# Opening of a fused attention and two-layer kernel: softmax sums of two units in column tiles spread by transfers, score banks paired, squares folded on GpSimd

## The chip, the core and the metric

The kernel runs on one core of a Trainium2 chip. Its engines work in parallel, each through its own instructions in order: TensorE (PE: matmuls; PEld: its weight loads), VectorE (DVE), ScalarE (ACT), GpSimd (POOL) and SyncE (SP, which here only starts transfers). Sixteen DMA engines move data; those transfers that SP starts stand in the profile as queue q1, those that GpSimd starts as q0. The metric is device time in microseconds (us); less is better.

## The reference

Attention over 8 batches and 12 heads, 448 rows of 64 each, with q and k normalized first; then a layer pair with a leaky rectifier between.

```python
q_n, k_n = rmsnorm(q, g_q), rmsnorm(k, g_k)        # x / sqrt(mean(x*x) + 1e-6) * g
scores = scale * np.matmul(q_n, k_n.transpose(0, 1, 3, 2))
scores = scores - np.max(scores, axis=-1, keepdims=True)
attn = np.exp(scores)
attn = attn / (np.sum(attn, axis=-1, keepdims=True) + 1e-09)
x = np.matmul(attn, v)          # then laid out as 3584 x 768
h = x @ w_in                    # 768 x 2048
out = np.maximum(0.01 * h, h) @ w_out   # 2048 x 768
```

## The kernel before

**Units.** The work is cut into 24 units of four heads, three units to a batch. A unit u goes through these steps, each a small function:

- `load(u)` (L146): q and k, 448 KB each, started by SP into `raw` tiles (three buffers); `load_v` (L149) v, `load_w_in` (L125) and `load_w_out` (L128) the weights, started by GpSimd, which also converts them to 16 bits.
- `prep_sqp` (L173) squares q and k on GpSimd (`prep_sq`, L169, on ScalarE), `prep_ssq` (L180) sums the squares of each row on VectorE, `prep_rinv` (L185, L186) makes 1/rms with Ln and Exp on ScalarE, `prep_norm` (L192) multiplies on VectorE.
- `tr` or `trn` (L861, L204) transposes on TensorE, with copies back by VectorE (L809, L811).
- `qk(u, steps)` (L222): seven score steps of four 64x64 matmuls, each into a pair of PSUM banks; `ex(u)` (L242) is the exponential of a step, from PSUM into the tile `et`, on ScalarE. It takes a shift, `eb`, so that nothing overflows: `shift_max` takes the maximum of step 0 on VectorE, `shift_mm` spreads it over the partitions with a matmul.
- `zsum`/`zsum_slot` (L300, L311) sum the exponentials with matmuls by ones, `zinv` turns the sums into reciprocals in the tile `rz` with Ln and Exp (L385, L387); `pv` (L401) multiplies the exponentials by v; `xmul` (L410) multiplies that by `rz` on VectorE and frees the banks of `pv`.
- For units 3 to 22 the sums are made in another form: `zcol` (L338) leaves them in four column tiles of 32 partitions, `zcol_ln` and `zcol_inv` (L359, L364) work on 224 columns into the tile `zs`, and four transfers of SP (L369) spread `zs` over the partitions of `rz`.

`zs` and `rz` come from `zpool`, which has one buffer of each; `zcol_ln` of the next unit writes the `zs` that the transfers before it read, and the next `rz` is the one that `xmul` before it reads.

**The order.** The schedule is manual: each engine gets its instructions in the order of the program. Units 0 to 2 are written out by hand (L828 to L1029), and this is the opening. From unit 3 on a loop interleaves the scores of a unit with matmuls of the two layers, from a plan. The eight PSUM banks are kept in a list: `slot` gives a pair of the banks 4 to 7 to a score step, `aux` a single one of the banks 0 to 3 (in the opening); `drop` gives them back. `warm(n, bank)` (L825) issues n matmuls of ones whose result nothing reads.

In the opening, between the score steps of unit 1 stand the sums and values of unit 0 (`zsum_slot(0)`, `pv(0)`, `zinv(0)`, `xmul(0)`) and the normalizing of unit 2; between those of unit 2 the same of unit 1 and unit 3. `pv(2)` takes the two banks that `pv(1)` had. `gate(u)` (L288) is a tiny copy on GpSimd that waits for the normalized k of unit u, so that what follows on GpSimd doesn't run ahead.

Of the kernel before, what the change touches and what calls it, by code (L numbers as in the profile page):

```python
# [8 lines left out]
FP32 = mybir.dt.float32  # L9
FP16 = mybir.dt.float16  # L10
AF = mybir.ActivationFunctionType
ALU = mybir.AluOpType
# [6 lines left out]
def kernel(  # L19
# [41 lines left out]
    def mine(i):  # L61
        return shared or i < 4

    def aux():
        can = [i for i in free if mine(i)]
        if shared:
            can = [i for i in can[:-1] if i ^ 1 not in free] or can
        free.remove(can[0])
        return single[can[0]]
# [12 lines left out]
    def drop(tile_):  # L82
        for i in range(8):
            if tile_ is single[i]:
                assert i not in free
                free.append(i)
                return
        x = [i for i in range(4) if tile_ is double[i]][0]
        assert 2 * x not in free and 2 * x + 1 not in free
        free.extend((2 * x, 2 * x + 1))  # L90
# [31 lines left out]
    def load_w_in(n0, n):  # L122
        for a in range(2):
            for r in range(2):
                nc.gpsimd.dma_start(win16[64 * a:64 * a + 64, :, r, n0:n0 + n], win_v[a, :, :, r, n0:n0 + n])  # L125
# [22 lines left out]
    def load_v(u):  # L148
        nc.gpsimd.dma_start(vts[u % NV].rearrange("p a t d -> p a (t d)"), rows(v, u))  # L149
# [9 lines left out]
    def buf(u, name):  # L159
        if name not in st[u]:  # L160
            shape, dtype, bufs = SHAPES[name]
            st[u][name] = prep_p.tile(shape, dtype, tag=name[:2] if bufs == 3 and name != "qkT" else name, bufs=bufs, name=name)
        return st[u][name]
# [7 lines left out]
    def prep_sqp(u, tis=BOTH):  # L171
        for ti in tis:
            nc.gpsimd.tensor_tensor(buf(u, f"sq{ti}"), raw[u][ti], raw[u][ti], op=ALU.mult)  # L173

    def prep_g(u):
        nc.vector.tensor_scalar(buf(u, "qkT")[:, 0], buf(u, "qkT")[:, 0], gcol, None, op0=ALU.mult)

    def prep_ssq(u, c=ALL, tis=BOTH):
        for ti in tis:
            nc.vector.tensor_reduce(buf(u, "ssq")[:, ti, :, c[0]:c[1]], buf(u, f"sq{ti}")[:, :, c[0]:c[1]],  # L180
                                    axis=AXL.X, op=ALU.add)

    def prep_rinv(u, tis=BOTH):
# [35 lines left out]
    def score(u, t, banks):  # L219
        for r in range(2):  # L220
            for a in range(2):
                nc.tensor.matmul(banks[a][64 * r:64 * r + 64, 0:S].rearrange("p (t x) -> p t x", t=NS),  # L222
                                 kT(u, r, a, t), qT(u, r, a), start=True, stop=True)

    def qk(u, steps):
        st[u]["sT"] = []
        for t in steps:
            sT = slot()
            score(u, t, (sT[:, 0], sT[:, 1]))
            st[u]["sT"].append((t, sT))  # L230

    def ex(u, most=NS):
        s = st[u]
        if "et" not in s:
            s["et"] = epool.tile([P, NS, 2, S], FP16, tag="et", name="et")
        for t, sT in s["sT"][:most]:
            if isinstance(sT, list):
                for a in range(2):
                    nc.scalar.activation(s["et"][:, t, a], sT[a][:, 0:S], AF.Exp, bias=s["eb"], scale=1.0)
                    drop(sT[a])  # L240
            else:
                nc.scalar.activation(s["et"][:, t], sT[:, :, 0:S], AF.Exp, bias=s["eb"], scale=1.0)  # L242
                drop(sT)
        s["sT"] = s["sT"][most:]

    def score0(u):
        banks = [aux() for a in range(2)]
        score(u, 0, banks)
        st[u]["sT"] = [(0, banks)]

    def shift_max(u):
        s = st[u]
        sT = s["sT"][0][1]
        if isinstance(sT, list):
            pm2 = small.tile([P, 2], FP32, tag="pm2", name="pm2")
            for a in range(2):
                nc.vector.tensor_reduce(pm2[:, a:a + 1], sT[a][:, 0:S], axis=AXL.X, op=ALU.max)
            s["spare"] = sT[0]
            nc.vector.tensor_reduce(s["spare"][:, 511:512], pm2, axis=AXL.X, op=ALU.max)
        else:  # L260
            s["spare"] = sT[:, 0]
            nc.vector.tensor_reduce(s["spare"][:, 511:512], sT[:, :, 0:S], axis=AXL.XY, op=ALU.max)  # L262
        s["dg"] = small.tile([P, P], FP16, tag="dg", name="dg")
        nc.vector.tensor_tensor(s["dg"], ident16, s["spare"][:, 511:512].broadcast_to([P, P]), op=ALU.mult)

    def shift_bank(u):
        st[u]["pb"] = aux()

    def shift_mm(u):
        s = st[u]  # L270
        if u > 0 and "pslot" in st[u - 1]:
            pb = st[u - 1]["pslot"][:, :, S:S + 64]
            for x in range(2):
                nc.tensor.matmul(pb[:, x], onesp, s["dg"][:, 64 * x:64 * x + 64], start=True, stop=True)  # L274
            nc.vector.tensor_reduce(s["spare"][:, 510:511], pb, axis=AXL.XY, op=ALU.max)  # L275
        else:
            if "pb" not in s:
                shift_bank(u)
            pb = s["pb"]
            nc.tensor.matmul(pb[:, 0:P], onesp, s["dg"], start=True, stop=True)  # L280
            nc.vector.tensor_reduce(s["spare"][:, 510:511], pb[:, 0:P], axis=AXL.X, op=ALU.max)
            if u >= 3:
                drop(pb)
        s["eb"] = small.tile([P, 1], FP32, tag="eb", name="eb")
        nc.vector.tensor_scalar(s["eb"], s["spare"][:, 510:511], -1.0, DELTA, op0=ALU.mult, op1=ALU.add)

    def gate(u):
        nc.gpsimd.tensor_copy(gate_t, buf(u, "n16")[:, 1, NS - 1, 1, D - 1:D])  # L288
# [534 lines left out]
    def warm(n, bank):  # L823
        for x in range(n):
            nc.tensor.matmul(bank[:, P:2 * P], onesp, onesp, start=True, stop=True)  # L825

    with tc.manual_schedule():
# [25 lines left out]
        prep_norm(0, K0, (1,))  # L853
        prep_norm(0, K1, (1,))

        def tr(u, ti, chunks, tp=None):
            if tp is None:
                tp = aux()
            for c, copy in chunks:
                for x in range(*c):  # L860
                    nc.tensor.transpose(as_tp(tp)[:, x, :], buf(u, "n16")[:, ti, x].rearrange("p a d -> p (a d)"), ident16)  # L861
                copy(buf(u, "qkT")[:, ti, c[0]:c[1]], as_tp(tp)[:, c[0]:c[1]], ti == 0)
            return tp
# [12 lines left out]
        gate(0)  # L876
        load_v(0)
        prep_sqp(2, (0,))
        load_v(1)
        load_v(2)  # L880
        load_w_in(0, 1024)
        shift_bank(0)
        warm(10, st[0]["pb"])
# [4 lines left out]
        def trn(u, ti, copy):  # L888
            prep_tr(u, ti, ((ALL, copy),))
# [14 lines left out]
        gate(1)  # L904
        prep_sqp(2, (1,))
        prep_sqp(3, (0,))
        load_w_in(1024, 1024)
        wb = aux()
        warm(12, wb)
# [3 lines left out]
        drop(wb)  # L913
        qk(0, (3,))
        ex(0)
        drop(tr(1, 0, ((ALL, vcopy),)))
        tpk = tr(1, 1, ((K0, vcopy),))
        qk(0, (4,))
        ex(0)
        k1 = []  # L920
# [3 lines left out]
        shift_max(1)  # L924
        vcopy(*k1[0])
        drop(tpk)
        shift_bank(1)
        qk(0, (5,))
        ex(0)
        warm(8, st[1]["pb"])  # L930
        qk(0, (6,))
        ex(0)
        warm(4, st[1]["pb"])
        shift_mm(1)
        prep_ssq(2, ALL, (1,))
        prep_ssq(3, ALL, (0,))
        ex(1)
        prep_rinv(2)
        qk(1, (1,))
        ex(1)  # L940
        zsum_slot(0)
        pv(0)
        zinv(0)
        prep_norm(2)
        gate(2)
        prep_sqp(3, (1,))
        load_v(3)
        load(5)
        prep_sqp(4, (0,))
        load_v(4)  # L950
        for f in range(2):
            load_w_out(8 * f, 8)
        qk(1, (2,))
        warm(6, st[1]["pb"])
        drop(st[1]["pb"])
        ex(1)
        trn(2, 0, vcopy)
        qk(1, (3,))
        ex(1)
        trn(2, 1, vcopy)  # L960
        xmul(0)
        qk(1, (4,))
        ex(1)
        qk(1, (5,))
        ex(1)
        score0(2)
        shift_max(2)
        qk(1, (6,))
        ex(1)
        shift_bank(2)  # L970
        warm(12, st[2]["pb"])
        shift_mm(2)
        prep_ssq(3, ALL, (1,))
        prep_ssq(4, ALL, (0,))
        ex(2)
        prep_rinv(3)
        qk(2, (1,))
        ex(2)
        zsum_slot(1)
        pv(1)  # L980
        zinv(1)

        prep_norm(3)
        load(6)
        gate(3)
        prep_sqp(4, (1,))
        prep_sqp(5)
        load_v(5)
        qk(2, (2,))
        ex(2)  # L990
        warm(12, st[2]["pb"])
        qk(2, (3,))
        ex(2)
        drop(st[2]["pb"])
        trn(3, 0, vcopy)
        warm(8, st[2]["pb"])
        trn(3, 1, vcopy)
        xmul(1)
        prep_ssq(4, ALL, (1,))
        qk(2, (4,))  # L1000
        ex(2)
        st[2]["zt"] = [aux() for r in range(2)]
# [14 lines left out]
        moe1_part(0, first, 0, 2)  # L1017
        shift_mm(3)
        xmul(2, (1,))
        push(0)  # L1020
        moe1_part(0, first, 2, KT - 2)
        ex(3)
# [147 lines left out]
```

## Time and profile before

| what | value |
|---|---|
| median of 3 runs | 409.96 us (408.93 to 411.95) |
| the profiled execution | 410.29 us, of it a span of 408.3 us from first to last instruction |
| PE, DVE, ACT, POOL busy | 395.0, 307.4, 301.4, 74.0 us |
| exponential of a score step (L242, 128x896) | 1.015 us, 166 times |
| Ln and Exp of the sums, wide (L385, L387) | 0.91 and 0.95 us, 3 times each |
| Ln and Exp of the sums, column tiles (L359, L364) | 0.36 and 0.40 us, 20 times each |
| sum of squares (L180, 128x896) | 1.07 us, 47 times |
| square on GpSimd (L173, 128x896) | 1.68 us, 14 times |
| q0, started by GpSimd | 11.80 MB |
| q1, started by SP | 50.08 MB |

A row of a chain or a timeline has the start in us from the span's beginning, the duration, the engine, the line of the kernel and what was made. A line of a queue has its packets, megabytes and the time that the packets took as a share of 16 engines. A line on transfers has the issuing engine, the number, the size of one, and the median time from issue to landing. A line on a stretch has its length, then busy time and instructions of the engine, the granted TensorE clock as a share of full speed, the DMA share and GB/s.

### The profile page before, as it was taken

The numbers are of one execution on the slowest core, as the hardware profiler recorded it, in microseconds if no ns is written. First come the engines' busy times: TensorE is split into PE (matmuls) and PEld (weight loads), VectorE is DVE, ScalarE is ACT, GpSimd is POOL, SyncE is SP. The second block draws the span as 40 slices with busy tenths as digits, with TensorE's granted clock in tenths as the row PEclk, the third lists the DMA queues.
The fourth block names the chain that finished last, engine by engine and source line by source line (L and its number), as shares of the span: only waits on it lengthen the run. The fifth ranks groups of instructions, "written<-read, shape, count | busy, mean of one in ns | idle before, by whom it ended". The sixth has DMA issues, their size and how long they took to land.

```text
span 408.3 us, 9444 instructions
## 1 busy us (share of the span) xinstructions
PE 395.0 (97%) x3834; PEld 222.9 (55%) x3834; DVE 307.4 (75%) x484; ACT 301.4 (74%) x476; POOL 74.0 (18%) x86
## 2 busy tenths in 40 slices
PE   7879999999999999999999999989999999999996
PEld 6545454555455544555455544555455557558963
DVE  5898789978888766876678857678579888567672
ACT  5998977879978599688878689868996667743600
POOL 1887331411020200120021200002011202000000
PEclk9899999999999999999999999999999999999999
DMA  5999999899665985578564984676652470032014
GB/s 178 270 251 254 239 236 247 212 204 181 164 161 100 244 218 102 149 196 183 145 158 50 246 218 99 172 176 174 177 96 47 122 163 8 15 72 77 2 39 117
DMA packets 72526, 62.87 MB, mean 154 GB/s; under 512 B 36388, under 2 KB 67620, under 8 KB 72484
## 3 DMA queue, kind: packets, MB, share of 16 engines
q1 hardware_dynamic: 61888, 50.08, 47.0%
q0 software_dynamic: 10272, 11.80, 18.6%
q8 instruction: 30, 0.49, 0.5%
q10 hardware_dynamic: 324, 0.39, 0.3%
q14 instruction: 12, 0.10, 0.1%
HBM read 45.61 MB, written 11.01 MB: 139 GB/s over the span
## 4 chain that ended last, share of the span: by engine, by line
PE 84%; DVE 6%; ACT 5%; DMA 2%; issue 2%; SPq 0%; DVEq 0%; ACTq 0%
PE banks L423 26%; PE banks L522 24%; PE banks L222 8%; PE banks L469 7%; PE banks L401 6%; PE banks L656 6%; PE banks L338 3%; ACT et L242 3%; DVE n L192 2%; DMA rz<-zs 1%; DMA rk<-in_k_dram 1%; PE banks L274 1%; ACT sq L169 1%; PE banks L204 1%; DVE xt L410 1%
## 5 line engine op out<-in xcount | busy, mean ns | idle before, releaser
L242 ACT ACTIVATE et<-banks,eb 128x896 f16<-128x896 f32 x166 | 160.0, 1015 | 23.4 <-PE banks L222 15.4
L423 PE MATMUL banks<-xt,win 128*128 128x448 f16 x612 | 122.2, 353 | 0.0
L423 PEld LDWEIGHTS <-win 128*128 128x128 f16 x612 | 57.3, 98 | 56.1 <-issue 6.8
L417 ACT ACTIVATE gt<-banks 128x448 f16<-128x448 f32 x104 | 56.6, 564 | 5.5 <-PE banks L423 4.4
L222 PE MATMUL banks<-qkT 64*64 64x448 f16 x672 | 49.6, 362 | 3.0 <-ACT et L242 2.1
L180 DVE TENSOR_REDUCE ssq<-sq 128x14 f32<-128x896 f32 (+2 forms) x49 | 50.1, 1056 | 1.3 <-ACT sq L169 1.1
L522 PEld LDWEIGHTS <-sa 128*128 128x128 f16 x352 | 33.4, 98 | 24.6 <-issue 3.6
L522 PE MATMUL banks<-tw,sa 128*128 128x384 f16 x264 | 46.8, 326 | 0.0
L529 DVE TENSOR_TENSOR ost<-banks,ost 128x384 f32<-128x384 f32 x55 | 30.3, 551 | 14.7 <-PE banks L522 14.1
L401 PE MATMUL banks<-et,vt 64*64 64x448 f16 x672 | 37.0, 349 | 0.1
L522 PEld LDWEIGHTS <-gt 128*128 128x128 f16 x264 | 25.5, 98 | 18.3 <-issue 1.7
L222 PEld LDWEIGHTS <-qkT 64*64 64x64 f16 x672 | 17.0, 105 | 32.5 <-issue 26.3
L469 PE MATMUL banks<-wout,gt 128*128 128x384 f16 x192 | 33.7, 326 | 0.0
L291 POOL COPY gate_t<-qkT 128x1 f16<-128x1 f16 x16 | 5.1, 321 | 152.6 <-DMA qkT<-n 152.6
L522 PE MATMUL banks<-wout,gt 128*128 128x384 f16 x176 | 32.4, 326 | 0.0
L379 POOL TENSOR_TENSOR xt<-x,rz 128x896 f16<-128x896 f32 x9 | 19.4, 2158 | 70.4 <-DMA rz<-zs 63.9
L262 DVE TENSOR_REDUCE banks<-banks 128x1 f32<-128x896 f32 x22 | 24.1, 1094 | 10.1 <-PE banks L222 6.3
L353 ACT COPY x<-banks 128x896 f32<-128x896 f32 x16 | 14.5, 906 | 22.1 <-DVE banks L275 22.1
L192 DVE TENSOR_TENSOR n<-rq,rinv 128x896 f16<-128x896 f32 (+2 forms) x25 | 28.3, 1137 | 1.3 <-ACT rinv L186 1.3
L192 DVE TENSOR_TENSOR n<-rk,rinv 128x896 f16<-128x896 f32 (+2 forms) x26 | 27.9, 1078 | 0.0
L401 PEld LDWEIGHTS <-vt 64*64 64x64 f16 x672 | 20.2, 107 | 10.6 <-issue 0.4
L469 PEld LDWEIGHTS <-gt 128*128 128x128 f16 x192 | 17.9, 98 | 13.7 <-issue 2.9
(105 smaller groups left out, 486.8 us busy)
## 6 DMA issues: line engine op xcount, KB each, us to landing
rq<-in_q_dram SPq DMA_DIRECT2D x24, 448.0 KB, 4.7
rk<-in_k_dram SPq DMA_DIRECT2D x24, 448.0 KB, 5.5
out_dram<-ost SPq DMA_DIRECT2D x52, 192.0 KB, 3.4
rz<-zs SPq DMA_DIRECT2D x80, 112.0 KB, 2.7
vt<-in_v_dram POOLq DMA_DIRECT2D x24, 224.0 KB, 4.9
win<-in_moe_w_in_dram POOLq DMA_DIRECT2D x8, 384.0 KB, 14.5
wout<-in_moe_w_out_dram POOLq DMA_DIRECT2D x2, 1536.0 KB, 29.0
out_dram<-ost SPq DMA_DIRECT2D x4, 96.0 KB, 2.1
```

Source lines behind the costliest of these rows:

```text
L180: nc.vector.tensor_reduce(buf(u, "ssq")[:, ti, :, c[0]:c[1]], buf(u, f"sq{ti}")[:, :, c[0]:c[1]], axis=AXL.X, op=ALU.add)
L192: nc.vector.tensor_tensor(buf(u, "n16")[:, ti, c[0]:c[1]].rearrange("p s a d -> p a s d"), src[:, :, c[0]:c[1]], buf(u, "rinv")[:, ti, :, ...
L222: nc.tensor.matmul(banks[a][64 * r:64 * r + 64, 0:S].rearrange("p (t x) -> p t x", t=NS), kT(u, r, a, t), qT(u, r, a), start=True, stop=True)
L242: nc.scalar.activation(s["et"][:, t], sT[:, :, 0:S], AF.Exp, bias=s["eb"], scale=1.0)
L262: nc.vector.tensor_reduce(s["spare"][:, 511:512], sT[:, :, 0:S], axis=AXL.XY, op=ALU.max)
L401: nc.tensor.matmul(s["pv"][r][64 * a:64 * a + 64, 0:S], vts[u % NV][64 * r:64 * r + 64, a, t], s["et"][64 * r:64 * r + 64, t, a], start=(t ...
L417: nc.scalar.activation(dst, src, AF.Prelu, bias=0.0, scale=1.0, alpha=0.01)
L423: nc.tensor.matmul(hps[:, 0:S], win16[:, kt // 2, kt % 2, ts(ft, P)], xt[:, kt // 2, kt % 2], start=(kt == 0), stop=(kt == KT - 1))
L469: nc.tensor.matmul(op2[:, 0:HC], gt[:, ft, ds(col(t), P)], wout16[:, ft, ds(HC * half, HC)], start=(i == 0), stop=(i == FT - 1))
L522: nc.tensor.matmul(bank[:, 0:HC], a[:, f], b[:, f], start=(first and f == 0), stop=(f == HF - 1), skip_group_check=not first)
L529: nc.vector.tensor_tensor(dst, g[name][:, 0:HC], src, op=ALU.add)
L656: nc.tensor.matmul(bank[:, HX * i:HX * i + HX].rearrange("p (t x) -> p t x", t=NS), w, x[:, kt], start=start, stop=(kt == HK - 1), skip_gr ...
```

## The change

- The sums of units 0 and 1 are made with `zcol`, `zcol_ln`, `zcol_inv` in place of `zsum_slot` and `zinv`. `zcol` of unit 0 and its Ln and Exp stand after the second score step of unit 1 is issued, `pv(0)` after the sixth; those of unit 1 stand after the second step of unit 2, with `xmul(0)` between its Ln and Exp, and `prep_norm(3)` after that.
- Step 0 of the scores of units 1 and 2 goes into a pair of the banks 0 to 3 in place of two single banks, so one exponential and one reduction cover it, and the shift is spread in columns of that same pair.
- A new `prep_fold` adds the two halves of the squares on GpSimd for unit 2 (q), 3 and 4; `prep_ssq` then reduces half as many elements.
- The k of unit 2 is copied back in two parts (row block 0 first, the rest after the first score step is issued), as for unit 1.
- `load_v(2)` moves behind `prep_fold(3)`; `load_v(4)` and `load_w_out` move from unit 1's steps to unit 2's; the `prep_ssq` of units 3 and 4 move one place later; 50 warming matmuls of units 1 and 2 become 20.

```diff
+    def pair():
+        x = [i for i in range(2) if 2 * i in free and 2 * i + 1 in free][0]
+        for i in (2 * x, 2 * x + 1):
+            free.remove(i)
+        return double[x]
...
+    def prep_fold(u, tis=BOTH):
+        for ti in tis:
+            sq = buf(u, f"sq{ti}")
+            nc.gpsimd.tensor_tensor(sq[:, :, :, 0:D // 2], sq[:, :, :, 0:D // 2], sq[:, :, :, D // 2:D], op=ALU.add)
+            folded.add((u, ti))
...
     def score0(u):
-        banks = [aux() for a in range(2)]
-        score(u, 0, banks)
-        st[u]["sT"] = [(0, banks)]
+        sT = pair()
+        score(u, 0, (sT[:, 0], sT[:, 1]))
+        st[u]["sT"] = [(0, sT)]
+        st[u]["own"] = sT
...
         shift_mm(1)
         prep_ssq(2, ALL, (1,))
-        prep_ssq(3, ALL, (0,))
         ex(1)
         prep_rinv(2)
         qk(1, (1,))
+        zcol(0)
+        zcol_ln(0)
+        zcol_inv(0)
         ex(1)
-        zsum_slot(0)
-        pv(0)
-        zinv(0)
         prep_norm(2)
         gate(2)
         prep_sqp(3, (1,))
+        prep_fold(3, (1,))
         load_v(3)
         load(5)
         prep_sqp(4, (0,))
+        qk(1, (2,))
...
+        qk(1, (5,))
+        ex(1)
+        pv(0)
+        qk(1, (6,))
+        ex(1)
+        shift_mm(2)
+        prep_ssq(3)
+        ex(2)
+        prep_rinv(3)
+        qk(2, (1,))
+        zcol(1)
+        zcol_ln(1)
+        xmul(0)
+        zcol_inv(1)
+        ex(2)
+        pv(1)
+        prep_norm(3)
+        load(6)
         load_v(4)
         for f in range(2):
             load_w_out(8 * f, 8)
...
-        zsum_slot(1)
-        pv(1)
-        zinv(1)
...
         xmul(1)
-        prep_ssq(4, ALL, (1,))
+        prep_ssq(4, ALL, (0,))
...
         xmul(2, (1,))
+        prep_ssq(4, ALL, (1,))
```

More of the change, by code (lines that the diff above doesn't have):

```diff
@@ L62, in mine, with aux @@
         return shared or i < 4
-    def aux():
-        can = [i for i in free if mine(i)]
+    def pair():
[3 more added lines that the diff above has]
+        return double[x]
+    def aux(bank=None):
+        can = [i for i in free if mine(i) and bank in (None, i)]
         if shared:
@@ L176, in prep_g @@
         nc.vector.tensor_scalar(buf(u, "qkT")[:, 0], buf(u, "qkT")[:, 0], gcol, None, op0=ALU.mult)
+    folded = set()
+    def prep_fold(u, tis=BOTH):
[3 more added lines that the diff above has]
+            folded.add((u, ti))
     def prep_ssq(u, c=ALL, tis=BOTH):
         for ti in tis:
-            nc.vector.tensor_reduce(buf(u, "ssq")[:, ti, :, c[0]:c[1]], buf(u, f"sq{ti}")[:, :, c[0]:c[1]],
+            w = D // 2 if (u, ti) in folded else D
+            nc.vector.tensor_reduce(buf(u, "ssq")[:, ti, :, c[0]:c[1]], buf(u, f"sq{ti}")[:, :, c[0]:c[1], 0:w],
                                     axis=AXL.X, op=ALU.add)
@@ L236, in ex @@
         for t, sT in s["sT"][:most]:
[L237 to L243, printed above, removed]
+            nc.scalar.activation(s["et"][:, t], sT[:, :, 0:S], AF.Exp, bias=s["eb"], scale=1.0)
+            drop(sT)
         s["sT"] = s["sT"][most:]
     def score0(u):
-        banks = [aux() for a in range(2)]
-        score(u, 0, banks)
-        st[u]["sT"] = [(0, banks)]
+        sT = pair()
+        score(u, 0, (sT[:, 0], sT[:, 1]))
+        st[u]["sT"] = [(0, sT)]
+        st[u]["own"] = sT
     def shift_max(u):
@@ L253, in shift_max @@
         sT = s["sT"][0][1]
[L254 to L262, printed above, removed]
+        s["spare"] = sT[:, 0]
+        nc.vector.tensor_reduce(s["spare"][:, 511:512], sT[:, :, 0:S], axis=AXL.XY, op=ALU.max)
         s["dg"] = small.tile([P, P], FP16, tag="dg", name="dg")
@@ L270, in shift_mm @@
         s = st[u]
-        if u > 0 and "pslot" in st[u - 1]:
-            pb = st[u - 1]["pslot"][:, :, S:S + 64]
+        peak = s["spare"][:, 510:511]
+        own = s.get("own")
+        if own is not None or u > 0 and "pslot" in st[u - 1]:
+            pb = (st[u - 1]["pslot"] if own is None else own)[:, :, S:S + 64]
             for x in range(2):
                 nc.tensor.matmul(pb[:, x], onesp, s["dg"][:, 64 * x:64 * x + 64], start=True, stop=True)
-            nc.vector.tensor_reduce(s["spare"][:, 510:511], pb, axis=AXL.XY, op=ALU.max)
+            if own is not None:
+                peak = small.tile([P, 1], FP32, tag="peak", name="peak")
+            nc.vector.tensor_reduce(peak, pb, axis=AXL.XY, op=ALU.max)
         else:
@@ L280, in shift_mm @@
             nc.tensor.matmul(pb[:, 0:P], onesp, s["dg"], start=True, stop=True)
-            nc.vector.tensor_reduce(s["spare"][:, 510:511], pb[:, 0:P], axis=AXL.X, op=ALU.max)
+            nc.vector.tensor_reduce(peak, pb[:, 0:P], axis=AXL.X, op=ALU.max)
             if u >= 3:
@@ L284, in shift_mm @@
         s["eb"] = small.tile([P, 1], FP32, tag="eb", name="eb")
-        nc.vector.tensor_scalar(s["eb"], s["spare"][:, 510:511], -1.0, DELTA, op0=ALU.mult, op1=ALU.add)
+        nc.vector.tensor_scalar(s["eb"], peak, -1.0, DELTA, op0=ALU.mult, op1=ALU.add)
     def gate(u):
@@ L854, with tr @@
         prep_norm(0, K1, (1,))
-        def tr(u, ti, chunks, tp=None):
+        def tr(u, ti, chunks, tp=None, bank=None):
             if tp is None:
-                tp = aux()
+                tp = aux(bank)
             for c, copy in chunks:
@@ L878 @@
         prep_sqp(2, (0,))
+        prep_fold(2, (0,))
         load_v(1)
-        load_v(2)
         load_w_in(0, 1024)
@@ L906 @@
         prep_sqp(3, (0,))
+        prep_fold(3, (0,))
+        load_v(2)
         load_w_in(1024, 1024)
@@ L915 @@
         ex(0)
-        drop(tr(1, 0, ((ALL, vcopy),)))
-        tpk = tr(1, 1, ((K0, vcopy),))
+        drop(tr(1, 0, ((ALL, vcopy),), bank=2))
+        tpk = tr(1, 1, ((K0, vcopy),), bank=3)
         qk(0, (4,))
@@ L926 @@
         drop(tpk)
-        shift_bank(1)
         qk(0, (5,))
         ex(0)
-        warm(8, st[1]["pb"])
+        wb = aux()
+        warm(8, wb)
         qk(0, (6,))
         ex(0)
-        warm(4, st[1]["pb"])
+        warm(4, wb)
+        drop(wb)
         shift_mm(1)
         prep_ssq(2, ALL, (1,))
-        prep_ssq(3, ALL, (0,))
         ex(1)
@@ L949 @@
         prep_sqp(4, (0,))
+        qk(1, (2,))
+        wb = aux()
+        warm(8, wb)
+        drop(wb)
+        ex(1)
+        drop(tr(2, 0, ((ALL, vcopy),), bank=2))
+        qk(1, (3,))
+        ex(1)
+        k1 = []
+        tpk = tr(2, 1, ((K0, vcopy), (K1, lambda *a: k1.append(a))), bank=3)
+        qk(1, (4,))
+        ex(1)
+        score0(2)
+        vcopy(*k1[0])
+        drop(tpk)
+        shift_max(2)
+        qk(1, (5,))
+        ex(1)
+        pv(0)
+        qk(1, (6,))
+        ex(1)
+        shift_mm(2)
[11 more added lines that the diff above has]
+        load(6)
         load_v(4)
@@ L952 @@
             load_w_out(8 * f, 8)
[L953 to L978, printed above, removed]
-        zsum_slot(1)
-        pv(1)
-        zinv(1)
-        prep_norm(3)
-        load(6)
         gate(3)
+        prep_fold(4, (0,))
         prep_sqp(4, (1,))
+        prep_fold(4, (1,))
         prep_sqp(5)
@@ L990 @@
         ex(2)
-        warm(12, st[2]["pb"])
         qk(2, (3,))
         ex(2)
-        drop(st[2]["pb"])
         trn(3, 0, vcopy)
-        warm(8, st[2]["pb"])
         trn(3, 1, vcopy)
         xmul(1)
-        prep_ssq(4, ALL, (1,))
+        prep_ssq(4, ALL, (0,))
         qk(2, (4,))
```

## The prediction

> **What bounds the kernel now.** I read the page's shares first, then the chain of waits.
>
> ```profile
> PE 395.0 (97%) x3834; PEld 222.9 (55%) x3834; DVE 307.4 (75%) x484; ACT 301.4 (74%) x476; POOL 74.0 (18%) x86
> DMA  5999999899665985578564984676652470032014
> PE 84%; DVE 6%; ACT 5%; DMA 2%; issue 2%; SPq 0%; DVEq 0%; ACTq 0%
> ```
>
> TensorE sets the time nearly everywhere, but the change lies in the opening, where the chain still runs over VectorE and ScalarE. And the DMA engines, averaging far below full, are full for slices 1 to 6 (10 to 71 us). The chain from 18 to 46 us:
>
> ```profile
> 21.45 1.16 ACT et L239 x2
> ...
> 23.97 0.81 ACT rz L385
> 24.81 0.95 ACT rz L387
> ...
> 36.76 1.07 DVE xt L410 x2
> 37.84 0.04 issue
> 37.88 0.76 PE banks L401 x10
> ...
> 43.66 0.54 PE banks L431 x2
> 44.20 1.89 PE banks L423 x10
> ```
>
> From 44.20 us on TensorE carries the chain. So the question is when the work that starts at 37.88, attention times values of unit 2 (pv(2)), can start. It waits for xmul(1) (L410), because pv(2) takes the banks of pv(1). Whatever moves xmul(1) moves the end.
>
> **Part by part, small edits.** The first score step: two exponentials of 0.63 us become one of 1.015 (L242), chain time 1.16 to about 1.0, twice: -0.3 us of ScalarE. The maximum: two reductions and a small one (1.15 + 0.17) become one (L262, 1.09): -0.2 each on VectorE. Bringing shift_mm and the k copy into this order leaves the instruction count as it is. The fold on GpSimd is not in the trace: a square of 128x896 takes 1.68 and a two-operand multiply 2.16 (L379), so half the size is between 0.84 and 1.08; I take 1.0. The reduction of half the elements is near the 128x384 and 128x512 rows (0.54, 0.69): 0.61 instead of 1.07, five times, -2.3 us of VectorE. GpSimd hides the folds: it gets to the third of them at about 28 us, done at 29.0, and VectorE asks for it at 29.1 to 29.6; if that cover went, ScalarE's reciprocal square root for unit 3 would be late by what is missing, some tenths. The later folds have over 2 us of slack. load_v(2) goes behind the fold and the square of unit 3, and its data between the two halves of w_in, which land from 30 us on; needed by pv(2) at 37.88: covered. load_v(4) and w_out come 1 to 2 us later into a software queue that is busy with w_in until about 40 us (23.5 + 16.5): nothing. pv(0) moves behind the sixth score step of unit 1 and puts 1.3 us of matmuls (L401, 28) ahead of the seventh; ScalarE waits some 0.4 us there, in the same stretch that the waits below cover. Thirty warming matmuls fewer (50 to 20) touch only the clock, below.
>
> **The sums.** Per unit, 28 matmuls of 64x64x448 (1.49 us) become 28 of 128x32x224 (the 20 at L338 take 0.73 in all, so 1.0), and Ln and Exp of 0.91 + 0.95 become 0.36 + 0.40: 1.1 us of ScalarE less, twice. In their place come four transfers each on SP, 448 KB, before xmul. This is the term that decides, so I walked the orders:
>
> 1. ScalarE: eb(1) is out at about 21.2; exponential, reciprocal root, Ln, Exp of unit 0 end at about 23.5. SP issues rz(0) from 23.5 at 0.6 us each, ahead of load(5).
> 2. VectorE, if nothing waits: maximum and shift of unit 2 by 29.1, two short reductions to 30.3, then xmul(0), now **ahead** of norm(3).
> 3. ScalarE at 30.9 wants Ln of unit 1 into zs. The pool of zs and rz has one buffer (bufs=1): that Ln waits until rz(0) has been read, and rz(1) is not issued until xmul(0) has run. Behind Ln on ScalarE stand all exponentials of unit 2; behind xmul(0) norm(3) and the transposes; TensorE's pv(1) waits for the bank of zcol(1).
>
> So when does rz land? The queue of SP, q1, in two stretches, 12 to 22 us and 22 to 30 us:
>
> ```profile
> rk<-in_k_dram SPq DMA_DIRECT2D x1, 448.0 KB, 12.4
> ```
> ```profile
> q0 software_dynamic: 591, 1.12, 74.0%
> q1 hardware_dynamic: 540, 0.91, 35.1%
> ...
> rq<-in_q_dram SPq DMA_DIRECT2D x1, 448.0 KB, 8.9
> rk<-in_k_dram SPq DMA_DIRECT2D x1, 448.0 KB, 12.1
> ```
>
> k of unit 4 is issued at 17.31 and lands at 29.7; q of unit 5, issued 24.46, at 33.4; its k, issued 25.46, at 37.6. They land in turn, 4 us apart: one line, full without a gap, sharing the engines packet by packet (540 against 591) with the weights on q0. rz(0), issued at 23.5, stands behind load(4) and ahead of load(5); rz(1) behind load(5). A unit's rz is 512 packets of 896 bytes (4 x 112 KB). Their pace, slow end: 540 packets in 8 us, 67.5 per us, 7.6 us. Fast end, where rz(3) itself moved, 64 to 66 us:
>
> ```profile
> q0 software_dynamic: 282, 0.24, 73.1%
> q1 hardware_dynamic: 301, 0.24, 46.4%
> ```
>
> 150 per us, 3.4 us, beside equally small packets. An engine spends 0.74 x 16 x 8 / 591 = 160 ns on a w_in packet, 83 on a load's, and by the last rows 49 on one of rz: rz beside w_in goes at 67.5 x 243 / 209 = 78 per us, 6.5 us; part of the way runs beside small v packets. I take **5.5**, bounds 3.4 and 7.6.
>
> Sum: rz(0) at 29.7 + 5.5 = 35.2 (VectorE and ScalarE have waited since 30.5); load(5) takes 37.6 - 29.7 = 7.9, to 43.1; rz(1) to 48.6; xmul(1), 1.15, to 49.8, where norm(3) and its copies (done about 43) no longer matter. pv(2) starts at 49.8 instead of 37.9: **+11.9**. The 1.4 us gained by 30 us is swallowed by the wait. From pv(2) to 44.2 the steps stay: scores 6, exponential, zinv(2), xmul(2). The reduction moved behind xmul(2) makes the reciprocal root of unit 4 0.3 late, off the chain.
>
> **The clock.** TensorE's stretches before and after 11 us:
>
> ```profile
> 7.50:11.00 3.50, 1.87 (x24) 0.98 0.89 319
> 11.00:14.30 3.30, 3.30 (x30) 0.50 1.02 360
> 14.30:17.70 3.40, 2.40 (x30) 1.00 1.16 249
> ```
>
> After 1.87 busy us of 3.5 the granted clock was 0.50 for 3.4 us. The waits for rz leave TensorE idle some 4 us before 35 and 4 before 49.8, so I expect 0.50 again as pv(2) starts. Twelve warming matmuls took 1.45 us there against 0.84; some 2.3 us of TensorE on the path to 44.2 and the first dense matmuls would stretch. I take +1.0; bounds 0 and 3.4 (two such stretches at half speed).
>
> The Trainium skill ("TensorE: Matmul & The Clock Gate", What's actually happening) asks for one idle window of about 3.4 us before the clock falls; the rows show it falling with more than half of the time busy. By the page alone this term would be 0 wherever a warming matmul lies in the window.
>
> The profiled run took 410.29 us, span 408.3; 410.29 + 11.9 + 1.0 = 423.2. The median of the runs is 0.33 lower: **422.9**. Bounds: fast rz (33.1, 41.0, 44.4, xmul to 45.6) and full clock, +7.7, 417.7; slow rz (37.3, 45.2, 52.8, to 54.0), +16.1, and 3.4 for the clock, 429.5.
>
> **Rivals.**
> (a) *The line doesn't hold.* rz passes the waiting loads, at the delay that rz(3) had on an empty q1 amid weights:
>
> ```profile
> q1 hardware_dynamic: 9, 0.01, 0.6%
> ...
> rz<-zs SPq DMA_DIRECT2D x4, 112.0 KB, 6.3
> ```
>
> (59 to 64 us: issued from 59.95, and 9 packets moved.) Then the last of rz(0), issued at 25.3, lands at 31.6; xmul(0) to 32.8; rz(1) issued to 34.6, landing 40.9, xmul(1) 42.1 against 37.83: +4.2, 414. The order of landings speaks against it.
> (b) *Faster.* Transfers land in the 2.7 us that is their median over the kernel: rz(0) at 28.0, before VectorE asks; rz(1) at 36.1, xmul(1) to 37.3, and the 2.2 us of ScalarE show in part: -0.6 to -2.5, 409 to 407.5. It turns from gain to loss where rz(1) lands after 36.7. Against it: 6.3 above, with nothing ahead.
> (c) *Longer.* Both transfers at the slow pace and the clock down for two stretches: 429 or more.
> (d) That the sums don't leave ScalarE can't be: the lines say it.
>
> The Trainium skill ("DMA: Bandwidth & Descriptors", Anatomy of one DMA) gives a fixed 2.0 us per transfer plus bytes at 436 GB/s, for transfers from GpSimd; an estimate by it for 448 KB is 3.1 us and the result would be (b). It counts no traffic ahead in the ring, and the 6.3 and 12.4 us here contradict it.
>
> **How the numbers follow.** Forecast (417.7 to 429.5) 0.72; (a) 0.13; (c) beyond 429.5 0.05; (b) 0.10, of it 0.03 over 1% faster and 0.07 within 1% (a measurement of this kernel tells no less from no change). The range reaches from just below (a) to the end of the bounds, 413 to 430. Slower by over 1% (above 414.1) is the forecast, (c) and all but 0.03 of (a): 0.87; within 1% 0.10; faster 0.03.
>
> **What would show it.** In the profile after: xmul at about 35 and 49 us released by DMA rz; Ln of zs at 31 to 35 us idle before, released by the same; k of load(5) landing 17 us after issue instead of 12; clock 0.50 somewhere in 35 to 55 us; the dense stage from 56 or 57 us, and the same durations after it. If xmul(1) ends before 38 us, the queue step is wrong; if it ends near 49 and the total is less than 8 us worse, later stages had room that I see none of.

## The result, and the profile after

The change makes the kernel slower: 424.69 us, the median of 6 runs (423.48 to 424.93), against 409.61 us for 6 runs of the kernel before beside it (408.74 to 411.95). The ratio is 1.0358, with a 95% interval of 1.0328 to 1.0388. Forecast were 422.9 us and a range of 413 to 430. The profiled execution took 424.9 us with a span of 422.8, which is 14.5 more span than before.

From the page of the kernel after: the shares, the granted clock in tenths for 40 slices of 10.6 us, and the chain by engine.

```profile
PE 399.4 (94%) x3806; PEld 225.2 (53%) x3806; DVE 307.4 (73%) x481; ACT 299.3 (71%) x474; POOL 80.8 (19%) x91
PEclk9886799999999999999999999999999999999999
...
PE 80%; DVE 8%; DMA 5%; issue 3%; ACT 2%; SPq 1%; DVEq 0%; ACTq 0%
```

ScalarE has 2 us less to do, as the change intends. VectorE is as busy as before: its sums of squares take 2.2 us less (47.9 instead of 50.1), but its multiplies of the normalizing 4.2 more (60.4 instead of 56.2), for a reason that the last section shows. What grew is the part of DMA in the chain (2% before, 5% now), and in slices 2 to 5 the clock is below nine tenths. The chain of waits of the kernel after, 18 to 62 us (start, us, engine, what, line):

```profile
25.18 0.65 SPq L377
...
27.16 8.92 DMA rz<-zs
...
36.18 0.37 ACT zs L367
...
36.98 0.53 SPq L377
...
38.85 9.36 DMA rz<-zs
...
48.33 0.64 DVE xt L418
...
49.01 1.33 PE banks L409 x10
...
56.96 2.27 PE banks L431 x12
```

This is the same stretch that before ran from the exponential at 21.45 over `xmul(1)` at 36.76 to the dense stage at 44.20. The two long rows are most of the loss: the transfers of unit 0 hold the chain for 9 us, then, because Ln of unit 1 (at 36.18) may not write `zs` before those have read it, the transfers of unit 1 for 9 more. The dense stage starts at 56.96, 12.8 us late. Of that, 11.1 are there when `pv(2)` starts (49.01 instead of 37.88), and 1.6 come between that and the dense stage (7.95 us instead of 6.32). The clock of those stretches, kernel after (stretch, length, PE busy and instructions, granted clock, DMA share, GB/s):

```profile
34.00:41.00 7.00, 4.41 (x43) 0.51 1.11 257
...
47.80:54.70 6.90, 5.69 (x52) 0.51 1.13 256
```

Towards the end of each long wait, at 34.2 and at 47.9, the clock falls to half for 6.9 us, and the second of these stretches covers `pv(2)` and what comes behind it.

The dense stage keeps this distance at first: the matmuls that spread the shift of unit 4 stand at 56.92 before and 69.68 after, 12.8 us apart. Those of unit 5 stand at 69.67 and 83.78, 14.1 apart. In between, the timeline of the kernel after shows the next loss (start, us, engine, line, operation, tiles, idle before and its releaser):

```profile
78.82 1.08 DVE L207 TENSOR_TENSOR n<-rq,rinv 128x896 f16<-128x896 f32 x1
78.95 2.49 POOL L179 TENSOR_TENSOR sq<-rq 128x896 f32<-128x896 f32 x1 [3.59 <-DVE ea L331]
79.82 2.57 DVE L207 TENSOR_TENSOR n<-rk,rinv 128x896 f16<-128x896 f32 x1
```

A square on GpSimd and the normalizing of VectorE meet; the square takes 2.49 instead of 1.68 us and the second multiply 2.57 instead of 1.08. The shift stands behind it, and TensorE waits 1.28 us for it at 83.78. So the sum is 11.1 + 1.6 + 1.4, and the remaining 0.4 up to 14.5 is there by unit 9, whose shift stands at 126.23 before and 140.75 after.

### The profile page after: what moved, and what is told of

It reads as the page before. It is cut to its first block, busy times and chain, and to the rows that moved or that the text cites. A ratio compares the mean times of both kernels' runs of the same rounds, so it can differ in the third digit from the quotient of the medians.

```text
span 422.8 us, 9405 instructions
## 1 busy us (share of the span) xinstructions
PE 399.4 (94%) x3806; PEld 225.2 (53%) x3806; DVE 307.4 (73%) x481; ACT 299.3 (71%) x474; POOL 80.8 (19%) x91
## 4 chain that ended last, share of the span: by engine, by line
PE 80%; DVE 8%; DMA 5%; issue 3%; ACT 2%; SPq 1%; DVEq 0%; ACTq 0%
PE banks L431 26%; PE banks L530 22%; PE banks L237 8%; PE banks L409 6%; PE banks L664 6%; PE banks L477 6%; DMA rz<-zs 5%; DVE n L207 2%; PE banks L346 2%; PE banks L833 2%; SPq L377 1%; DVE banks L266 1%; PE banks L280 1%; PE banks L439 1%; DVE ssq L195 1%
## 5 line engine op out<-in xcount | busy, mean ns | idle before, releaser
L252 ACT ACTIVATE et<-banks,eb 128x896 f16<-128x896 f32 x168 | 162.3, 1015 | 37.6 <-PE banks L237 26.9
L237 PE MATMUL banks<-qkT 64*64 64x448 f16 x672 | 51.7, 372 | 1.7 <-ACT et L252 1.1
L409 PE MATMUL banks<-et,vt 64*64 64x448 f16 x672 | 40.8, 367 | 8.6 <-DVE xt L418 5.4
L195 DVE TENSOR_REDUCE ssq<-sq 128x14 f32<-128x896 f32 (+3 forms) x49 | 47.9, 1009 | 0.7 <-ACT sq L175 0.7
L530 PEld LDWEIGHTS <-sa 128*128 128x128 f16 x352 | 33.4, 98 | 24.8 <-issue 3.9
L266 DVE TENSOR_REDUCE banks<-banks 128x1 f32<-128x896 f32 x24 | 26.3, 1096 | 16.9 <-PE banks L237 13.6
L477 PE MATMUL banks<-wout,gt 128*128 128x384 f16 x192 | 33.7, 326 | 0.0
L207 DVE TENSOR_TENSOR n<-rq,rinv 128x896 f16<-128x896 f32 (+2 forms) x25 | 31.9, 1278 | 1.3 <-ACT rinv L201 1.3
L409 PEld LDWEIGHTS <-vt 64*64 64x64 f16 x672 | 21.9, 111 | 20.3 <-issue 9.9
L361 ACT COPY x<-banks 128x896 f32<-128x896 f32 x16 | 14.5, 907 | 22.4 <-DVE banks L283 22.3
```

Source lines behind the costliest of these rows:

```text
L207: nc.vector.tensor_tensor(buf(u, "n16")[:, ti, c[0]:c[1]].rearrange("p s a d -> p a s d"), src[:, :, c[0]:c[1]], buf(u, "rinv")[:, ti, :, ...
L409: nc.tensor.matmul(s["pv"][r][64 * a:64 * a + 64, 0:S], vts[u % NV][64 * r:64 * r + 64, a, t], s["et"][64 * r:64 * r + 64, t, a], start=(t ...
L477: nc.tensor.matmul(op2[:, 0:HC], gt[:, ft, ds(col(t), P)], wout16[:, ft, ds(HC * half, HC)], start=(i == 0), stop=(i == FT - 1))
L530: nc.tensor.matmul(bank[:, 0:HC], a[:, f], b[:, f], start=(first and f == 0), stop=(f == HF - 1), skip_group_check=not first)
```

## The experiments

The theory: the transfers of `rz` cost the time, through what they wait for in the DMA engines, and the parts of the change without transfers cost about nothing. The rivals: the new order, the folds or the clock cost a good part by themselves; and, within the transfers, that it is the line on SP (transfers behind loads) against the share of the engines and a delay before a queue starts. Where a kernel is described as an edit of "after", everything else of the change stays.

**Wide sums back (e1).** After, with the sums of units 0 and 1 again by `zsum_slot` and `zinv`; no transfers in the opening.

```diff
-        zcol(0); zcol_ln(0); zcol_inv(0)
+        zsum_slot(0); zinv(0)
...
-        zcol(1); zcol_ln(1); xmul(0); zcol_inv(1)
+        zsum_slot(1); xmul(0); zinv(1)
```

> The changed kernel with the wide sums of the kernel before put back for units 0 and 1 (zsum_slot, and Ln and Exp on 896 columns; no transfers); all else of the change stays. Theory (the transfers are late, and VectorE, ScalarE and TensorE wait for them): pv(2) starts at 37 to 40 us instead of 49.0, total 408 to 412. Rival (the rest costs it: folds on GpSimd, fewer warming matmuls with the clock at half, the later values of unit 0): total 420 or more.

Measured: 412.9 us (411.61 to 415.05), ratio 1.008 (1.0049 to 1.0111). So 11.8 of the 15.1 us are the column sums with their transfers, and the theory holds, at 0.9 us over its upper end. Some 3 us stay. In the chain of waits of e1:

```profile
33.93 0.95 ACT rz L395
...
36.74 0.68 DVE qkT L817
...
45.39 2.27 PE banks L431 x12
```

`zinv(1)` stands ahead of the next exponential on ScalarE here, so the scores behind that, the transposes of unit 3 and their copies (at 36.74; 35.30 before) come late, and the dense stage starts 1.2 us late without any transfer. The span of this execution is 1.7 us longer than before's; what makes the rest of the 3 us isn't shown.

**Column sums alone (e2).** Before, with only the column sums and transfers of units 0 and 1, at the places where the sums stood.

```diff
-        zsum_slot(0)
+        zcol(0); zcol_ln(0)
...
-        zinv(0)
+        zcol_inv(0)
...
-        zsum_slot(1)
+        zcol(1); zcol_ln(1)
...
-        zinv(1)
+        zcol_inv(1)
```

> The kernel before with only the sums of units 0 and 1 in column tiles, spread by the four transfers of SP each; nothing else of the change. Theory: rz of unit 0 lands 9 to 11 us after its issue, xmul of unit 1 at 45 to 50 us instead of 36.7, total 418 to 424. Rival (the rest of the change costs it): total 408 to 411.

Measured: 427.79 us (2 runs), ratio 1.0439 (1.0392 to 1.0486). This is longer than expected, and the part alone costs more than the whole change, which at least places the sums earlier. VectorE in e2, the first half of `xmul` of unit 0 (in brackets the idle time before and its releaser):

```profile
33.00 0.62 DVE L410 TENSOR_TENSOR xt<-banks,rz 128x448 f16<-128x448 f32 x1 [7.00 <-DMA rz<-zs]
```

The second half follows only at 36.27. The wait of 7 us stands ahead of everything that VectorE has to do for unit 2 in the old order; the transfers of unit 1 are issued only at 42.56, the second half of `xmul(1)` follows at 53.20, and the dense stage starts 17.8 us late.

**Another ring (e3).** After, with those eight transfers started by ScalarE, on a queue that holds no loads.

```diff
-    nc.sync.dma_start(s["rz"][:, r, HS * y:HS * y + HS], src.broadcast_to([32, 4, HS]))
+    (nc.scalar if u < 2 else nc.sync).dma_start(s["rz"][:, r, HS * y:HS * y + HS], src.broadcast_to([32, 4, HS]))
```

> The changed kernel with the eight transfers of units 0 and 1 started by ScalarE, on a ring of its own, not behind the loads on that of SP. Theory, the line of loads: rz of unit 1 lands some 3 us sooner (45 instead of 48.2), total 420 to 422. Rival, the packets' share of the engines and the delay of a queue that starts decide: rz of unit 1 lands at 47 or later, total within 1.5 us of the changed kernel or longer.

Measured: 425.77 us (2 runs), ratio 1.0378 (1.0314 to 1.0442), the same as the change. The transfers take 8.2 us (unit 0) and 8.0 us (unit 1), in the median, to land with nothing ahead of them in their queue. The transfers of e3 from 24 to 28 us (those of unit 0 are issued from 25.05 on):

```profile
q0 software_dynamic: 329, 0.61, 81.1%
q1 hardware_dynamic: 217, 0.36, 27.9%
...
rz<-zs ACTq DMA_DIRECT2D x4, 112.0 KB, 8.2
```

ScalarE's queue, q10 in this profile, has no line there: it moved no packet yet, while q1 moved 217 beside the weights. So the line on SP is not needed for the loss: here my reading falls, and the share of the engines with the delay before a queue starts is enough. Issuing costs ScalarE 2.9 and 2.7 us as well, so how much the line adds is not measured cleanly by this run.

**Part of the weights later (e4).** After, with the second half of `w_in` issued behind the transfers of unit 1.

```diff
         load_v(2)
-        load_w_in(1024, 1024)
...
         load(6)
+        load_w_in(1024, 1024)
         load_v(4)
```

> The changed kernel with the second half of w_in (1.5 MB) started after the transfers of unit 1 instead of ahead of those of unit 0, so that the queue of GpSimd is almost empty when SP starts rz of unit 0. Theory, contention with the weights: rz of unit 0 lands 3 to 5 us after issue, rz of unit 1 at 36 to 41 us, total 409 to 415. Rival, the single ring of SP (loads of unit 5 ahead of rz of unit 1) is enough by itself: rz of unit 1 stays at 45 or later, total 420 or more.

Measured: 422.22 us, ratio 1.0303 (1.0275 to 1.0331), 2.5 us less than the change, and little of that is the edit's. Up to 24.8 us this execution has no stretch at half clock, and the transfers of unit 0 are issued at 23.50 instead of 25.18. The run doesn't answer its question: the first half of `w_in` and v still filled q0 from 20.0 to 28.3 us (624 packets, 76.2% of the engines), so unit 0's last transfer landed at 33.7, 10.2 us after the first was issued (10.9 in the change), and unit 1's then met the second half of `w_in` together with `w_out` and landed 10 us after the last of them was issued.

**Both halves after (e11).** After, with both halves of `w_in` issued only when k of unit 3 is normalized; v of unit 4 and `w_out` come behind them.

```diff
-        load_w_in(0, 1024)
...
-        load_w_in(1024, 1024)
...
+        gate(3)
+        load_w_in(0, 1024)
+        load_w_in(1024, 1024)
         load_v(4)
...
-        gate(3)
```

> The changed kernel with both halves of w_in started by GpSimd only after the normalized k of unit 3 (behind the transfers of unit 1), so that the queue of GpSimd carries nothing but v while rz of units 0 and 1 moves. Theory, the transfers are late because the weights' packets share the engines and hold back a queue that starts: the last rz of unit 0 lands 2.5 to 4 us after its issue instead of 9, rz of unit 1 by 38, pv(2) starts at 36.5 to 39 instead of 49.0, total 408 to 413. Rival, the single buffer and the order on SP are enough for the delay: pv(2) at 43 or later, total 417 or more.

Measured: 425.07 us, ratio 1.0349 (1.0301 to 1.0397). The total misses the expectation, and the first transfers meet it. The transfers of e11 from 20 to 30 us (queue: packets, megabytes, share; then issuing engine, count, size, median us to landing):

```profile
q0 software_dynamic: 272, 0.23, 18.4%
...
rz<-zs SPq DMA_DIRECT2D x4, 112.0 KB, 2.3
```

With few weights on the engines the same four transfers land in 2.3 us instead of 7 to 9, on the same queue. In both kernels q1 moves nothing else when they are issued, so for unit 0 this shows the cause: the weights on the engines. But `w_in` is now issued from 34.35, while the transfers of unit 1 are issued (33.08 to 36.5), and those take 7.8 us again; the dense stage starts 8.9 us late. Then a transposing transfer of unit 6 takes 9.7 us from 77.06, while q0 still moves 557 packets from 77 to 82; VectorE waits 4.7 us for it and TensorE 3.0, and the total is back at +15. That the later weights cause this is likely and not shown. **The same without folds (e12)**, where all `prep_fold` are taken out of e11:

> The kernel of e11 without the five folds on GpSimd (VectorE sums all 896 squares again). Theory, a fold with two inputs holds up VectorE's two-input multiply beside it and is paid for on the chain: 0.5 to 1.5 us less than e11. Rival, the folds save VectorE time that counts (0.47 us each, five of them): 0.5 to 2 us more than e11.

Measured: 424.22 us, ratio 1.0328 (1.0275 to 1.0382). `xmul(1)` ends at 39.7, only 1.9 us later than before, and now TensorE waits for `w_in` itself, 4.0 us. The dense stage starts at 51.92, and the total doesn't differ clearly from e11's. Column sums with a quiet queue *and* weights in time were not reached by any of these.

**TensorE kept busy in the wait (e6).** After, with a hundred warming matmuls ahead of `pv(2)`.

```diff
+        idle = slot()
+        warm(100, idle[:, 0])
+        drop(idle)
         pv(2, 0, 3)
```

> The changed kernel with 100 warming matmuls put into TensorE's wait ahead of pv(2). Theory, the clock term: the stretch from 49.0 to 57.0 us shortens from 8.0 to the 6.3 of the kernel before, total 1.3 to 2.0 us less than the changed kernel, about 423. If the clock term is wrong: within 0.5 us of the changed kernel.

Measured: 420.72 us, ratio 1.0272 (1.0238 to 1.0305), 4.0 us less than the change, by matmuls that nobody reads. The chain of waits of e6:

```profile
42.26 5.69 PE banks L833 x100
47.95 0.79 PE banks L409 x12
...
54.25 2.27 PE banks L431 x12
```

From `pv(2)` to the dense stage it takes 6.30 us instead of 7.95, which is before's 6.32: the 1.65 us between them are the clock. Another 1.06 us are there when `pv(2)` starts, from transfers issued and landing sooner. And 1.3 come because the square and the normalizing meet in the other order at 77 us: the multiplies come first and take 1.08 each, the square waits and takes 2.41, and the matmuls that spread the shift stand at 79.73 and wait for nothing. That is the 4.0, but only the 1.65 can be put down to the edit. The first transfers are issued 0.7 us sooner (24.51 instead of 25.18) for a reason ahead of it: the normalizing of unit 1 ends at 17.0 instead of 17.7, as it starts 0.4 us sooner (14.28) and loses 0.6 us to a fold already running instead of 0.9 to one that starts with it.

**Wide sums, no folds (e8).** e1 with all five `prep_fold` calls taken out, the reductions back at full width.

> The kernel of e1 (wide sums, no transfers) without the five folds. If the folds' collision with the normalizing of unit 1 (1.75 instead of 1.08 us in e1) is what is left of the loss, total 409 to 411.5 against 412.9 of e1; if the loss of e1 lies in the order of the steps, unchanged within 0.7 us.

Measured: 412.72 us, ratio 1.0071 (1.0038 to 1.0103), the same as e1. The folds as a whole save nothing and cost nothing there: the normalizing of unit 1 is no longer held up, and instead two reductions of 2.07 us together stand ahead of `xmul(0)`, which Ln of unit 1 follows. The dense stage is at 47.1, but this execution has about half clock from 38 to 42 us (0.58 and 0.57) where that of e1 has none, so the two profiles don't settle more than the totals do.

**Wide sums in the old order (e17).** e1 with the sums' Ln and Exp behind the next exponential, as before, and without the fold of unit 2.

```diff
-        zsum_slot(0); zinv(0); ex(1)
+        zsum_slot(0); ex(1); zinv(0)
...
-        zsum_slot(1); xmul(0); zinv(1); ex(2)
+        zsum_slot(1); xmul(0); ex(2); zinv(1)
...
-        prep_fold(2, (0,))
```

> The kernel of e1 (wide sums, no transfers) with two edits: the Ln and Exp of a unit's sums stand after the second exponential of the next unit, as in the kernel before, not ahead of it; and the fold of unit 2, which ran against the normalizing of unit 1, is left out. Theory on the 1.2 us by which the dense stage of e1 begins late (45.4 against 44.2): the order costs it, since in e1 the transposes of unit 3 wait behind a score step that those 1.9 us hold up, and the fold costs 0.7; then the dense stage begins at 43.5 to 44.3 and the total is 409 to 411, 2 to 3 less than e1. Rival, the rest of the change (values of unit 0 later, fewer warming matmuls) costs it: 412 or more.

Measured: 410.25 us, ratio 1.0014 (0.9994 to 1.0034): no difference from the kernel before that can be measured. So the 2.7 us between this and e1 are the order together with that one fold, and since leaving out all folds (e8) changed nothing, mostly the order; that is argued, and the order was not run alone. The chain of waits of e17 shows more:

```profile
42.20 2.27 PE banks L431 x12
...
66.21 7.93 DMA qkT<-n
```

The dense stage starts 2.0 us **sooner** than before, and then all of it is given back: a transposing transfer (`qkT` of unit 6), issued at 66.21, lands only at 74.1, VectorE waits 2.06 us for it, and the matmuls that spread the shift of unit 6 stand at 81.67, where before they stood at 81.66.

**A load moved behind that transfer (e18).** e17, with the load of unit 8 issued behind the transposing transfer instead of ahead.

```diff
-    if u + 4 < NU: job(load, u + 4)
+    if u + 4 < NU and u != 4: job(load, u + 4)
...
     job(prep_trd, u + 2)
+    if u == 4: job(load, u + 4)
```

> The kernel of e17 with the load of unit 8 started after the transposing transfer of unit 6 instead of ahead of it on SP. In e17 the dense stage began 2.0 us sooner than in the kernel before, and all of it was lost at 74 us, where VectorE waited for that transfer (issued 66.2, landed 74.1). Theory, the line on SP's ring (load of unit 8 landed at 69 and 71): the transfer lands at 71 or sooner, most of the 2.0 us is kept, total 408.0 to 409. Rival, the engines are full with the weights until about 68 us whatever stands in line: it lands at 73 or later, total 410 or more.

Measured: 410.55 us, ratio 1.001 (0.9987 to 1.0034). The transfer lands at 72.4, 1.7 sooner, so the load was part of its wait. But then VectorE's steps behind it run beside GpSimd's and are held up, TensorE waits 1.4 us for the shift, and the gain is gone again. The total is the rival's, and the landing is neither's (71 or sooner, 73 or later).

**Paired banks alone (e13).** Before, with only the paired first score steps of units 1 and 2 and the shift in that pair.

```diff
-        banks = [aux() for a in range(2)]
+        banks = pair()
```

> The kernel before with only the paired first score step of units 1 and 2 (one exponential, one maximum, the shift in columns of the same pair). By the sums of the prediction: 0.3 us less on ScalarE and 0.4 less on VectorE; total 0.2 to 0.8 us less than the kernel before, about 409.2. Rival, the pair is not free as early as two single banks and the step waits: 0.5 us or more longer.

Measured: 408.52 us (408.29 to 410.34, 12 runs), ratio 0.9968 (0.9951 to 0.9985), faster than both kernels by a little. The dense stage starts at 43.60 instead of 44.20, and at the shift of unit 6 the 0.6 us are still there (81.05 instead of 81.66). Against the median of before beside it, 410.41 in 23 runs, it is 1.9 us, more than expected; between the fastest runs of the two it is 0.4 (408.29, 408.70). Of the parts that were run without the rest, it is the only one that helps.

**Before once more (e0).** The unchanged kernel, for what differs between two executions of it.

> The kernel before, unchanged, for a second profile. If the place where the granted clock falls in the opening (10.9 to 14.3 us in the first profile, 17 to 24 in the changed kernel) is a matter of the execution, the fall stands somewhere else here or is missing; if the change moved it, it stands at 10.9 again.

Measured: 410.28 us, span 408.3. Two stretches of TensorE in this second profile:

```profile
10.80:14.30 3.50, 2.30 (x34) 1.00 1.04 367
...
17.80:21.30 3.50, 3.50 (x31) 0.51 1.05 190
```

In the first profile it is the stretch from 11.0 that has half the clock (0.50) and the one from 17.7 full speed; e13 has none at half clock. So where the clock falls in the opening, up to 24 us, differs between executions of one kernel, and e4, which has the same program as the change up to there, has no fall in it. That the change has no part in its own fall from 17.1 to 24.0 is not shown. A fall towards the end of a wait for `rz`, or just behind it, is in every kernel that leaves TensorE idle there (0.50 in e2, e3, e4, e11, e12 and the first wait of e6).

## Why the prediction was right, and where its steps were not

The number was 1.8 us short of the median and the cause the one named: `xmul(1)`, released by the transfers, moves `pv(2)` and everything behind it. That it came so near is partly luck. Against the 12.9 us forecast the span grew by 14.5: 0.8 less up to `pv(2)`, 0.6 more by the clock, and 1.8 later on that were not in the sum. By its steps:

- **The single buffer, and who waits behind it.** Right. ScalarE stands idle for 3.54 us ahead of Ln of unit 1, until the transfers of unit 0 have read `zs`; those of unit 1 are issued at 36.98, and `xmul(1)` ends at 48.95 (49.8 forecast). `pv(2)` starts 11.1 us late (11.9 forecast).
- **"rz(0), issued at 23.5, stands behind load(4)".** This step failed, though its landing, 36.1 (35.2 forecast), was nearly met; it was issued at 25.18. k of unit 4 landed at 26.8 and not at 29.7: q0 moved 325 packets from 17.8 to 21.8 us, where it was 464 before, and q1 275 instead of 103 (`load_v(2)`, which now comes later, would explain it; that was not tried alone). So q1 was nearly empty as rz(0) came. What held it is shown in the transfers of the kernel after from 25.9 to 30 us:

```profile
q0 software_dynamic: 400, 0.73, 104.8%
q1 hardware_dynamic: 30, 0.03, 2.4%
```

  Four us with 30 packets moved on q1, none of them before 28.2, then 613 from 30 to 36.2, with those of load(5) among them. This is the mechanism of rival (a), a start from an empty queue amid weights, in the place where I had the line; e3 (another queue, 8.2 us all the same) and e11 (same queue, few weights, 2.3 us) show that it suffices. I priced (a) at 414 because I took the 6.3 us of rz(3) for both units; here it is 9 us to the last landing, amid packets of 1.8 KB (0.73 MB in 400) where rz(3) had 0.85 KB (0.24 in 282). Two wrong parts nearly cancelled: no line, and a longer delay. That the landing was met is luck.
- **rz(1) behind load(5).** As forecast: k of load(5), issued at 29.28, landed at 44.2, 15 us later (17 forecast), and rz(1) at 48.2 (48.6 forecast). Whether rz(1) would have been faster without load(5) stays open; with nothing ahead, on ScalarE's queue, it took 8.0.
- **The clock, +1.0.** Right in kind, too small: 1.63, and e6 measures 1.65. I reckoned with 3.4 us at half speed, from the one drop in the trace; the drops here last 6.9. The one idle window of about 3.4 us that the Trainium skill ("TensorE: Matmul & The Clock Gate", What's actually happening) asks for stands ahead of one fall here, that at 47.9, behind a gap of 3.84 us. At 34.2 the clock fell after only 0.8 us without a matmul, and at 17.1 with no gap over 0.6 us in the 5 us ahead and 2.03 us busy of the last 3.4, so the rows still go further than that rule. More work in the wait (e6) kept the clock up there.
- **"GpSimd hides the folds."** Not all. A fold takes 1.13 (0.84 to 1.08 were my bounds), and that of unit 2 takes 2.07 and holds up the normalizing of unit 1 (1.16 becomes 2.04), in the first score step's chain. Together with half clock from 17 to 24 us, this put the shift of unit 1 out at 22.9; I had forecast 21.2, and before it was 21.4. The waits behind, which I had swallow what is gained or lost by 30 us, passed this on: where the transfers of unit 0 were issued 0.7 us (e6) and 1.7 us (e4) sooner, the last landed 0.95 and 2.4 sooner, and `pv(2)` started 1.1 and 1.8 sooner.
- **"The same durations after it."** Missing in the sum: +1.4 at 80 us, where GpSimd's square met VectorE's normalizing. The opposite also holds: e17 gained 2.0 us in the opening, and a transfer from 66 to 74 us took it back. The distance between two traces is not rigid behind an opening.

## What to carry to other kernels

Replacing 2 us of engine work by a transfer that is needed at once is priced by what the DMA engines carry in that stretch: the same four transfers took 2.3 us amid little traffic and 9 amid weights, and the stretch must be looked up, not the median of the kernel. A tile with one buffer, written by the next unit's step, turns one such wait into two in a row. And where a stage is bound by a chain of latencies, a gain that lands on a transfer later on, or a wait that lets the clock drop, is only settled by following the distance between the two traces to the end.

## What the runs showed of the hardware

- **GpSimd's two-operand instructions and VectorE's multiplies of two SBUF operands exclude each other.** At 14.67 us of the kernel after, a multiply of 1.08 runs at its own pace, the fold that starts with it takes 2.07 (1.13 alone, so it waited 0.94), and the next multiplies, started at 15.72, end 1.02 us after the fold. The lines of the timeline:

```profile
14.67 1.08 DVE L207 TENSOR_TENSOR n<-rq,rinv 128x896 f16<-128x896 f32 x1
14.67 2.07 POOL L189 TENSOR_TENSOR sq<-sq 128x448 f32<-128x448 f32 x1
15.72 2.04 DVE L207 TENSOR_TENSOR n<-rk,rinv 128x128 f16<-128x128 f32 x2
```

  The Trainium skill ("SBUF — State Buffer", SBUF: two separate sides) says that the two share a port pair, that whichever starts first has it for the whole instruction, and that the other blocks; these rows and those at 79 us agree, and so does e6 at 77, where VectorE is first and GpSimd waits. It speaks against the folds, because the reductions that they shorten read one operand: two of them from 12.69, beside a square, took their usual 2.07. The trace of before had it too: a normalizing of 2.39 at 228.76, beside a GpSimd multiply.
- **A queue that starts from empty amid a full q0 moves almost nothing for some 3 to 4 us**: 30 packets from 25.9 to 30 here, 9 from 59 to 64 before, and none up to 28 of what ScalarE issued from 25.05 on in e3, beside a running q1. Where q0 is light (18.4% of the engines in e11) the same transfers land in 2.3 us. How the 9 us divide between that delay and the sharing of the engines was not separated.
- **The clock falls at different places in two executions of the same kernel** (from 11.0, from 17.8, for 3.4 us each), and the one profile of e13 has no such fall.
